# Thresholded attention and a GELU layer on one core: conversion steps made whole, and the first weight loads moved behind the rows of pair two

## The chip, the cores and the metric

The kernel runs on one core of a Trainium2 chip. Time is the device time of one execution in microseconds (us), and kernels are compared by the median of their runs. TensorE is called PE, and PEld where it loads weights; VectorE is DVE, ScalarE is ACT, GpSimd is POOL. SyncE is SP: it only issues transfers here. Each of ACT, POOL and SP has a DMA queue of its own.

## What is computed

The inputs are q, k and v of shape (8, 8, 576, 64) in single precision, a threshold tau, and two weight matrices, 512 x 2048 and 2048 x 512. The weights come in double precision, eight bytes a number.

```
scores = q @ k^T / 8
keep scores that are >= max(scores) - tau, the others count as -1e9
attn = exp(scores - max); attn /= (sum(attn) + 1e-9)
x = (attn @ v), heads side by side: 4608 tokens x 512
out = gelu(x @ w_in) @ w_out, gelu exact
```

## The kernel before, in words

The attention works on pairs of heads: 32 pairs, four to each of the eight batches. The 576 queries of a pair go in five slots: four chunks of 128, and one for the last 64 queries of both heads. So a batch of four pairs has 20 slots. The first batch has an order of its own: first the chunks 0 and 1 of all four pairs (slots 0 to 7), then the chunks 2, 3 and the rest, pair by pair (slots 8 to 19).

What a slot does, in the order in which it is written:

1. `scores` (L410): matmuls of queries and keys into two score banks in PSUM, one for each head. There are only two of them, so the next slot's scores wait for this slot's masking.
2. `softmax_head`: for each head the maxima (L422, DVE), the threshold from them (L425, POOL) and the exponentials (L427, ACT). Between the first maxima and the first threshold, `add_low_bits(True)` puts one addition of converted weights (L226, POOL), the newest that is due. After `softmax_head` a plain `add_low_bits()` puts the others.
3. `turn_qk_early`, in slots 0, 2 and 4: the next pair's q and k are turned by PE (L326, and L336 for the last rows) and copied by ACT (L329 to L343).
4. Sums with v of an earlier slot (L546, L570), their division, and in the second half of the batch first matmuls of the big layers (L638).
5. `turn_p_early` (L356, L363, L372): the masked exponentials of the slot before are turned.
6. `softmax_tail` (L443, DVE): masking by the threshold and the row sums, in one operation.
7. Loads that are due, and `convert`, with a budget in ns for this slot's share of weight conversion.

Weights come as 32 pieces of 512 columns, 512 KB each as they lie in memory. `load_piece` (L183) issues the load of the next piece. It goes to a slot of `xall` or, for every other piece, to a part of `turned_p`. Each piece takes these steps from double to single precision: ACT makes `power` from the high words (L202) and a part of the result from the low words (L203); DVE shifts `power` (L210) and brings in the sign (L212); POOL adds the two (L226). `conversions` is a generator that issues these steps, ACT's two pieces ahead of DVE's, and yields what each costs in ns. `convert` adds 1200 (slots 1 and 2) or 1900 ns (later slots) to a debt and takes steps until the debt is used up; slot 19 takes all that are left. As written, the generator yields 340 after L210 and 720 after L212, and only after that second yield is the piece entered in `sums_due`, from which `add_low_bits` takes, and the next load issued.

At the start, `load_early` loads q and k of the pairs 0, 1 and 2: q on the SP queue, k of pair 0 on ACT's, of pair 1 on POOL's, and all of pair 2 on SP's, into slots of `xall`. The rows 512 to 575 of a pair are loaded apart, as a tail. Pieces 0 and 1 follow pair 0's k on ACT's queue, pieces 2 and 3 pair 1's k on POOL's. `load_v_early` and `load_early(3)` then load pair 0's v, pair three's q and k, and pair 1's v on SP's queue. After `turn_qk_early(0)` the generator is started, with ACT's first two steps.

After the first batch, PE alternates between attention and the big layers in an order laid down by `goal` and `fill`; the last ten blocks of tokens are multiplied at the end in a scheme with fewer products (L826).

Of the kernel before, what the change touches and what calls it, by code (L numbers as in the profile page):

```python
# [18 lines left out]
def kernel(  # L19
# [28 lines left out]
    nc = tc.nc  # L48
# [53 lines left out]
    def x_slot(want=None):  # L102
        i = max(x_free) if want is None else want
        x_free.remove(i)
        return i
# [8 lines left out]
    def x_rows(i):  # L114
        return xall[:, i, :, :].rearrange("p c t -> p (c t)")
# [45 lines left out]
    def load_piece(eng=nc.sync):  # L161
        k = loaded[0]
        if k == len(pieces):
            return
        staged = k % 2 and k < len(pieces) - LATER
        if wide and not staged and not x_free:
            return
        dst, src = pieces[k]
        loaded[0] += 1
        if not wide:  # L170
            nc.sync.dma_start(dst, src)
            converted[0] += 1
            load_piece()
            return
        slot = []
        if staged:

            half, at = divmod(k // 2 % 4, 2)
            raw = pd[half].bitcast(U32)[:, at * 2 * PIECE:(at + 1) * 2 * PIECE]
        else:  # L180
            slot = [x_slot()]
            raw = x_rows(slot[0]).bitcast(U32)
        eng.dma_start(raw, src.bitcast(U32))  # L183
        raws.append((dst, raw, slot))

    def conversions():

        vec = nc.vector
        ahead = []
        done = 0
        while raws or ahead:
            if raws:
                dst, raw, slot = raws.pop(0)
                lo, hi = (raw.rearrange("p (f w) -> p f w", w=2)[:, :, i] for i in range(2))  # L200
                power = gp.tile([P, PIECE], U32, tag="g", name="power")
                nc.scalar.activation(power.bitcast(FP32), hi.bitcast(FP32), AF.Copy, bias=0.0, scale=2.0 ** -112)  # L202
                nc.scalar.activation(dst.bitcast(U32), lo, AF.Copy, bias=0.0, scale=2.0 ** -29)  # L203
                ahead.append((dst, hi, power, slot))
                yield 0
            if len(ahead) == LATER and done == len(pieces) - LATER:
                yield None
            if len(ahead) == 2 or not raws:
                dst, hi, power, slot = ahead.pop(0)
                vec.tensor_scalar(power, power, 3, 0x7FFFFFF8, op0=ALU.logical_shift_left, op1=ALU.bitwise_and)  # L210
                yield 340
                vec.scalar_tensor_tensor(power, hi, 0x80000000, power, op0=ALU.bitwise_and, op1=ALU.bitwise_or)  # L212
                x_free.extend(slot)
                yield 720
                sums_due.append((dst.bitcast(U32), power))
                load_piece()
                done += 1
                yield 0

    sums_due = []  # L220

# [7 lines left out]
    conv = {"steps": None, "debt": 0.0}  # L229

    def convert(ns, least=0):

        if conv["steps"] is None:
            conv["steps"] = conversions()
        conv["debt"] += ns
        while conv["debt"] > 0 or least > 0:
            took = next(conv["steps"], None)
            if took is None:
                return
            conv["debt"] -= took  # L240
            least -= took
# [31 lines left out]
    def load_early(p):  # L273
        b, hp = divmod(p, HP)
        s = st[p] = {}
        for name, src in (("q", q), ("k", k)):

            if p == 2:
                at = s[name + "_slot"] = x_slot()
                t = x_rows(at)[:, 0:2 * (NC + 1) * D].rearrange("p (e c d) -> p e c d", e=2, d=D)  # L280
            else:
                t = ld.tile([P, 2, NC + 1, D], FP32, tag=name, name=name)
            s[name] = t
            eng = (nc.scalar, nc.gpsimd)[p] if p < 2 and name == "k" else nc.sync
            for e in range(2):
                rows = src[b, 2 * hp + e, 0:MAIN, :]
                if name == "q":
                    eng.dma_start(t[:, e, 0:NC, :].rearrange("p (g c) d -> p g (c d)", c=2),
                                  rows.rearrange("(g p c) d -> p g (c d)", p=P, c=2))
                else:  # L290
                    eng.dma_start(t[:, e, 0:NC, :], rows.rearrange("(p t) d -> p t d", p=P))
            eng.dma_start(t[0:TAIL, :, NC, :], src[b, 2 * hp:2 * hp + 2, MAIN:S, :].rearrange("e s d -> s e d"))

    def load_v_early(p):
        b, hp = divmod(p, HP)
        t = st[p]["v"] = v_sb[p % 4]
        for e in range(2):
            nc.sync.dma_start(t[:, e, 0:NC, :], v[b, 2 * hp + e, 0:MAIN, :].rearrange("(p t) d -> p t d", p=P))
            nc.sync.dma_start(t[e * TAIL:(e + 1) * TAIL, e, NC, :], v[b, 2 * hp + e, MAIN:S, :])
# [735 lines left out]
        assert not beside  # L1035

    load_early(0)
    for _ in range(2):
        load_piece(nc.scalar)
    some = const.tile([P, 1], FP32, name="some")  # L1040
    nc.vector.tensor_scalar(some, tau_sb, 0.0, None, op0=ALU.is_ge)
    nc.vector.tensor_scalar(q_scale, some, SCALE, None, op0=ALU.mult)
# [2 lines left out]
    nc.vector.tensor_scalar(tau_eff, tau_sb, lift, None, op0=ALU.max)  # L1045
    nc.scalar.activation(warm[:, 1:2], warm[:, 0:1], AF.Exp)
    load_early(1)
    for _ in range(2):
        load_piece(nc.gpsimd)
    load_early(2)  # L1050
    for t in q_tail + [t[:, :, NC, :] for t in v_sb]:
        nc.vector.memset(t, 0.0)
    turn_qk_early(0)
    conv["steps"] = conversions()
    next(conv["steps"])
    load_v_early(0)
    load_early(3)
    load_v_early(1)
# [167 lines left out]
```

## Time and profile before

| | before |
|---|---|
| median of 3 runs | 1341.14 us (1337.87 to 1342.4) |
| profiled execution | 1338.39 us |
| its span | 1336.6 us |
| PE busy | 1318.4 us |
| DVE busy | 1042.8 us |
| ACT busy | 604.7 us |
| POOL busy | 640.2 us |
| L210, 32 in the first 140 us | 16.8 us, 525 ns each |
| L212, 32 in the first 140 us | 26.8 us |
| L226, 32 in the first 140 us | 42.5 us |

Busy time is summed over the span. A line of the timeline gives the start in us, the duration in us, the engine, the line of the kernel, the operation, what it writes and reads, the shape, the count, and in brackets the engine's idle time before it and what ended it. An end that is written as "DMA" is a landing transfer. In a table by stage, each engine's busy time is followed by the number of its instructions, and the last columns are the granted PE clock as a share of full speed, the mean busy share of the DMA engines, and GB/s.

### The profile page before, as it was taken

How to read it: one execution, taken by the hardware profiler on the slowest of the kernel's cores; microseconds unless marked ns; L12 is line 12 of the kernel's file. 1: busy time of each engine (PE TensorE's matmuls, PEld its weight loads, DVE VectorE, ACT ScalarE, POOL GpSimd, SP SyncE). 2: the span in 40 equal slices, each digit the busy share in tenths (PEclk: the TensorE clock that was granted, in tenths of full speed). 3: DMA queues.
4: the chain of work that ended last, by engine and by line, in shares of the span. 5: the costliest groups of instructions: out<-in, count | busy, mean ns of one | idle time of the engine just before them, and what ended most of it. 6: DMA issues, size and time to landing. Idle time of an engine off the chain costs nothing.

```text
span 1336.6 us, 19968 instructions
## 1 busy us (share of the span) xinstructions
PE 1318.4 (99%) x6362; PEld 895.1 (67%) x6362; DVE 1042.8 (78%) x2005; ACT 604.7 (45%) x1029; POOL 640.2 (48%) x1063
## 2 busy tenths in 40 slices
PE   8899999999999999999999999999999999999998
PEld 6677466466466466466466557568787787877877
DVE  6977777788888888888888888783857698386775
ACT  7877457268367358348448438332211113211120
POOL 4655454555555555546545551235264503635530
PEclk9999999999999999999999999999999999999999
DMA  7662566776776786786786775400000130000003
GB/s 234 211 171 50 124 151 141 168 184 152 176 188 151 180 202 153 179 211 154 168 222 159 163 188 121 106 9 1 1 0 1 40 103 17 0 1 0 1 0 79
DMA packets 209784, 152.42 MB, mean 114 GB/s; under 512 B 113360, under 2 KB 193088, under 8 KB 209680
## 3 DMA queue, kind: packets, MB, share of 16 engines
q1 hardware_dynamic: 191680, 125.11, 39.7%
q0 software_dynamic: 17280, 24.69, 6.8%
q10 hardware_dynamic: 720, 1.34, 0.3%
q8 instruction: 52, 0.85, 0.3%
q14 instruction: 52, 0.43, 0.1%
HBM read 55.97 MB, written 12.52 MB: 51 GB/s over the span
## 4 chain that ended last, share of the span: by engine, by line
PE 93%; DMA 2%; ACT 2%; DVE 2%; issue 0%; SPq 0%; DVEq 0%; ACTq 0%
PE bank L826 34%; PE o_ps L653 17%; PE hT L638 16%; PE sc L410 13%; PE xT L546 11%; ACT p L427 1%; DMA xall<-in_moe_w_in_dram 1%; DMA q<-in_q_dram 1%; DMA x<-xall 0%; DVE nmx L422 0%; PE tr L356 0%; DVE power L212 0%; ACT pT L363 0%; DVE power L210 0%; DVE p L443 0%
## 5 line engine op out<-in xcount | busy, mean ns | idle before, releaser
L427 ACT ACTIVATE p<-sc,nmx 128x576 f32<-128x576 f32 x288 | 201.7, 738 | 276.6 <-DVE nmx L422 276.4
L443 DVE SCALAR_TENSOR_TENSOR p<-sc,thr,p 128x576 f32<-128x576 f32 x288 | 225.2, 815 | 74.3 <-ACT p L427 70.2
L425 POOL TENSOR_SCALAR thr<-nmx,tau_eff 128x1 f32<-128x1 f32 x288 | 84.2, 293 | 355.8 <-DVE nmx L422 347.0
L638 PE MATMUL hT<-xall,w_in 128*128 128x256 f32 x1024 | 241.9, 386 | 0.0
L422 DVE TENSOR_REDUCE nmx<-sc 128x1 f32<-128x576 f32 x288 | 205.3, 749 | 45.0 <-PE sc L410 43.5
L653 PE MATMUL o_ps<-w_out,g 128*128 128x512 f32 x512 | 236.8, 603 | 0.0
L638 PEld LDWEIGHTS hT<-xall,w_in 128*128 128x128 f32 x1024 | 189.4, 190 | 50.1 <-issue 23.0
L708 DVE TENSOR_TENSOR c<-c,bank 128x320 f32<-128x320 f32 x304 | 146.9, 486 | 34.0 <-PE bank L826 20.6
L708 DVE TENSOR_TENSOR o<-o,bank 128x256 f32<-128x256 f32 x240 | 99.6, 418 | 93.8 <-PE bank L826 88.8
L653 PEld LDWEIGHTS o_ps<-w_out,g 128*128 128x128 f32 x512 | 93.1, 190 | 109.1 <-issue 106.5
L410 PE MATMUL sc<-kT,qT 64*128 64x288 f32 x960 | 159.5, 429 | 2.0 <-DVE p L443 1.9
L546 PE MATMUL xT<-pT,v 128*64 128x320 f32 (+1 forms) x1240 | 159.6, 410 | 0.7 <-DVE pT L367 0.5
L507 DVE STREAM_TRANSPOSE turned_p<-p 128x1152 f32<-128x1152 f32 x112 | 154.4, 1378 | 3.9
L410 PEld LDWEIGHTS sc<-kT,qT 64*128 64x128 f32 x960 | 91.5, 186 | 74.9 <-issue 60.9
L546 PEld LDWEIGHTS xT<-pT,v 128*64 128x64 f32 x1240 | 86.5, 137 | 71.5 <-issue 10.8
L826 PE MATMUL bank<-w_out,c 128*128 128x256 f32 x480 | 120.2, 381 | 0.5 <-DVE o L708 0.5
L269 POOL DMA_DIRECT2D v<-in_v_dram x208 | 110.8, 536 | 3.8 <-issue 1.7
L826 PEld LDWEIGHTS bank<-w_out,c 128*128 128x128 f32 x480 | 90.0, 190 | 18.7 <-DVE o L708 2.9
L879 ACT ACTIVATE c<-c 128x320 f32<-128x320 f32 (+1 forms) x80 | 46.9, 624 | 114.6 <-DVE c L708 114.5
L708 POOL TENSOR_TENSOR c<-c,g 128x320 f32<-128x320 f32 (+1 forms) x40 | 50.6, 1272 | 67.5 <-DVE c L708 67.5
L826 PE MATMUL bank<-t_out,c 128*128 128x256 f32 x320 | 82.8, 381 | 0.0
L826 PE MATMUL bank<-t_out,g 128*128 128x256 f32 x320 | 82.1, 379 | 0.0
(182 smaller groups left out, 1771.5 us busy)
## 6 DMA issues: line engine op xcount, KB each, us to landing
pT<-turned_p SPq DMA_DIRECT2D x448, 160.0 KB, 3.5
pT<-pd_tail SPq DMA_DIRECT2D x112, 80.0 KB, 2.9
q<-in_q_dram POOLq DMA_DIRECT2D x104, 72.0 KB, 3.4
k<-in_k_dram POOLq DMA_DIRECT2D x104, 72.0 KB, 2.9
inv<-turned SPq DMA_DIRECT2D x54, 128.0 KB, 3.9
v<-in_v_dram POOLq DMA_DIRECT2D x156, 40.0 KB, 3.1
out_dram<-o SPq DMA_DIRECT2D x40, 128.0 KB, 2.3
xall<-in_moe_w_out_dram SPq DMA_DIRECT2D x9, 512.0 KB, 4.3
```

Of the source, the lines that this page charges most:

```text
L269: eng.dma_start(t[r:P:4, e, 0:n, :], rows[:, r * KR:r * KR + n, :])
L410: nc.tensor.matmul(sc[e][:, h, 0:HALF], lhsT=lhsT, rhs=s["kT"][rows, at:at + HALF], start=True, stop=True)
L422: nc.vector.tensor_reduce(nmx[:, e:e + 1], sc, axis=AXIS.XY, op=ALU.max, negate=True)
L425: nc.gpsimd.tensor_scalar(thr[:, e:e + 1], nmx[:, e:e + 1], -1.0, tau_eff, op0=ALU.mult, op1=ALU.subtract)
L427: nc.scalar.activation(w[:, e * S:(e + 1) * S].rearrange("p (h s) -> p h s", h=2), sc, AF.Exp, bias=nmx[:, e:e + 1], scale=1.0)
L443: nc.vector.scalar_tensor_tensor(row, sc[e][:, :, 0:HALF], thr[:, e:e + 1], row, op0=ALU.is_ge, op1=ALU.mult, accum_out=den[e])
L507: nc.vector.transpose(turned_p[:, :, i // 2, 0:NB, i % 2 * Q:(i % 2 + 1) * Q], w.rearrange("p (e b i) -> p e b i", e=2, i=Q))
L546: nc.tensor.matmul(to, lhsT=s["v"][:, e, c, :], rhs=rhs, start=(c == 0), stop=(c == KR - 1))
L638: nc.tensor.matmul(hT[:, j % 2, :], lhsT=w_in_sb[c][:, j * P:(j + 1) * P], rhs=x_blk[n][:, c, :], start=(c == 0), stop=(c == N_DM - 1))
L653: nc.tensor.matmul(o[:, 0:d_model], lhsT=g[j][:, m * P:(m + 1) * P], rhs=w_out_sb[j], start=(j == 0), stop=(j == N_DF - 1))
L708: eng.tensor_tensor(out, a, b, op=ALU.add)
L826: nc.tensor.matmul(to, lhsT=l, rhs=r, start=start and k == 0, stop=k == len(pairs) - 1, skip_group_check=not start)
```

## The change

Two things are changed. In `conversions`, L210 and L212 of a piece form one step of 1060 ns, and the piece is entered in `sums_due`, and the next load issued, before the generator yields. At the start, the first four pieces are loaded on SP's queue, after pair two's rows, and the generator is no longer started there: its first steps come with `convert` in slot 1.

```diff
             if len(ahead) == 2 or not raws:
                 dst, hi, power, slot = ahead.pop(0)
                 vec.tensor_scalar(power, power, 3, 0x7FFFFFF8, op0=ALU.logical_shift_left, op1=ALU.bitwise_and)
-                yield 340
                 vec.scalar_tensor_tensor(power, hi, 0x80000000, power, op0=ALU.bitwise_and, op1=ALU.bitwise_or)
                 x_free.extend(slot)
-                yield 720
                 sums_due.append((dst.bitcast(U32), power))
                 load_piece()
                 done += 1
-                yield 0
+                yield 1060
...
     load_early(0)
-    for _ in range(2):
-        load_piece(nc.scalar)
...
     load_early(1)
-    for _ in range(2):
-        load_piece(nc.gpsimd)
     load_early(2)
+    for _ in range(4):
+        load_piece(nc.sync)
     for t in q_tail + [t[:, :, NC, :] for t in v_sb]:
         nc.vector.memset(t, 0.0)
     turn_qk_early(0)
-    conv["steps"] = conversions()
-    next(conv["steps"])
     load_v_early(0)
     load_early(3)
     load_v_early(1)
```

## The prediction

> **What bounds the kernel now.** I read the chain of waits first (93% TensorE), then busy time by stage, because the change touches only the first attention batch and the start.
>
> ```profile
> PE 93%; DMA 2%; ACT 2%; DVE 2%; issue 0%; SPq 0%; DVEq 0%; ACTq 0%
> ```
>
> By stage:
>
> ```profile
> 0.00:75.00 75.00, 65.82 (x557) 49.72 (x557) 59.13 (x132) 60.70 (x128) 41.28 (x66) 0.98 0.68 222
> ...
> 75.00:140.00 65.00, 62.44 (x388) 46.27 (x388) 48.18 (x98) 51.53 (x102) 33.92 (x56) 1.00 0.38 86
> 140.00:876.00 736.00, 735.09 (x3516) 439.59 (x3515) 624.72 (x1123) 402.26 (x616) 371.35 (x758) 1.00 0.71 165
> ```
>
> The rows are stage, length, busy time of PE, PEld, DVE, ACT, POOL, clock, DMA share, GB/s. TensorE is idle 9.2 us of the first 75, 2.6 us of the next 65, and 0.9 us of the 736 after that. Its instructions have the same order in both kernels. So whatever is gained or lost before 140 us reaches the end one for one, and only about 12 us of idle time, and what a lowered clock adds, is to be had. That is the frame of the forecast.
>
> Then the timeline of the first 75 us. Slots are numbered by their maxima (L422): slot 2 at 19.11, 6 at 44.02, 7 at 50.40, 8 at 55.41, 11 at 71.84.
>
> ```profile
> 8.40 0.33 PE L336 MATMUL tr<-ident,q 64*64 64x64 f32 x4 [1.44 <-DMA q<-in_q_dram]
> ...
> 10.00 0.66 ACT L202 ACTIVATE power<-xall 128x512 f32<-128x512 f32 x1
> 10.57 0.65 ACT L203 ACTIVATE w_in<-xall 128x512 uint32<-128x512 uint32 x1
> 11.24 1.37 ACT L427 ACTIVATE p<-sc,nmx 128x576 f32<-128x576 f32 x2
> ```
>
> The first scores wait 1.44 us for the tail rows of pair 0's q, and piece 0 is converted on ACT while ACT has little else.
>
> ```profile
> 41.79 1.29 POOL L226 TENSOR_TENSOR w_in<-power,w_in 128x512 uint32<-128x512 uint32 x1 [0.72 <-DVE power L212]
> ...
> 41.93 1.45 DVE L210 TENSOR_SCALAR power<-power 128x512 uint32<-128x512 uint32 x1 [0.22 <-ACT power L202]
> ...
> 48.42 1.32 POOL L226 TENSOR_TENSOR w_in<-power,w_in 128x512 uint32<-128x512 uint32 x1 [0.79 <-DVE power L212]
> ...
> 48.65 1.66 DVE L212 SCALAR_TENSOR_TENSOR power<-turned_p,power 128x512 uint32<-128x512 uint32 x1
> ```
>
> And the stages around the gap that follows:
>
> ```profile
> 46.00:48.00 2.00, 1.57 (x7) 1.58 (x8) 1.97 (x6) 2.00 (x7) 1.38 (x2) 0.62 0.51 180
> 48.00:50.00 2.00, 2.00 (x11) 1.37 (x9) 1.97 (x3) 1.74 (x4) 1.32 (x1) 0.53 0.31 66
> ```
>
> L210 usually takes 0.42 and L212 0.69. When an addition on POOL started just before, they take 1.45 and 1.66, and end with it. TensorE is idle from 44.09 to 46.42, and its clock is then 0.62 and 0.53.
>
> [...] L210 and L212 stretch as shown, while maxima under an addition (55.41) keep their 0.7 us. [...] The trace shows 0.53 after a gap of 2.33 us, and 1.00 after gaps of 1.34 and 1.44 us (73.1, 6.96). [...] pair 0's q tail needed some 6.6 us from issue to landing beside the pieces on two other queues, pair three's on the SP queue alone 3.5 us.
>
> **The change part by part.**
>
> *(a) Pieces 0 to 3 leave the ACT and POOL queues and enter SP's behind pair two.* ACT loses issues of 0.60 and 0.41 us; its table load (4.95) can start near 2.4. POOL loses 0.58 and 0.56 where it waits until 11.05 anyway: worth nothing. The q tail, issued at 1.75, should land near 1.75 + 3.5 = 5.3, at worst as today, 8.4. Below 7.0 it no longer matters, since TensorE turns k until 6.96. Then the tail turns at 7.0, the kT copy ends at 7.69 as now, the held-back scores run at 8.05 instead of 9.38, maxima at 8.85 instead of 10.18. The exponentials now start as soon as the first maximum is done: 9.62 instead of 11.24, 1.6 us earlier, of which ACT's copies for pair one keep 1.5. Pair one's q, which landed at 11.0, must be there by 9.25; with 2 MB fewer bytes beside it I take that as given.
>
> SP issues four more pieces, some 2.1 us, before pair 0's v, pair three's q and k, and pair one's v. These are needed at 24.18 and 29.72 and today were issued by 12.3 and 21.6: covered, unless over 3 us slower. SP's own issues sum to about 10 us up to the last piece; 2.1 MB at the 350 GB/s seen at 10 to 14 us then take 6 us. So the pieces land between about 11 and 17 us (an estimate from these rates). They are needed from 16.3 on, one each 1.15 us: just covered. Two later pieces move ahead of pair three's v and of pair four's rows; those are used over 10 us after they land.
>
> *(b) Piece 0's conversion moves behind slot 0.* On ACT, L202 and L203 (0.58 us each in sequence) leave 10.0 to 11.2, where only about 0.3 us of them delayed anything, counted in (a), and join slot 1, where ACT is busy without a break from 15.39 to 27.3. DVE gets a fourth operation there: L210 and L212 of piece 1 must follow its L202. Before slot 2: L202 of piece 1 ends 19.65, L210 19.7, L212 20.15, maxima 20.75, exponentials 21.45, all less 1.5, so 19.95 instead of 20.08. **Start and delay cancel: 0.1 us gained.**
>
> *(c) Whole steps.* No slot ends between L210 and L212 any more, and an addition enters at once. So the newest addition follows the slot's last L212, under the maxima. Counting the 340, 720 and 1060 through the slots: before, the newest addition ran into an L210 or L212 in slots 6, 7, 11, 12, 15 and 17, for 1.03, 0.97, 1.00, 0.96, 0.49 and 0.96 us; after, in none. Price: the addition (1.3 us) starts 0.23 after the maxima do, so the threshold (0.3) behind it is ready at 1.85 and the masking (L443) starts at 1.90 instead of 1.63 in most slots: 0.27 each. Behind the masking wait DVE's next conversions and TensorE's next scores, which need its score banks. Slots 2, 8, 13 and 18 get an L212 from the slot behind, 0.61 late there, given back one to five slots on. The second addition of a slot falls under the masking, and ends about when L210 follows (3.4 after the maxima); it costs up to 0.2, taken as 0. L473 still stretches an L210 by 0.3 to 0.5 as today.
>
> Following the dependences by slot, with 1.48 from masking start to the next conversion and 1.06 per step: ACT's 0.35 us wait for a piece at 30.92 goes, since that piece is issued sooner. Maxima of slot 6 at 44.02 - 0.45 - 1.03 = 42.54. Masking 44.44, two steps, slot 7 at 48.03 instead of 50.40; TensorE's gap shrinks to about 1 us, so the lowered clock should not come, and today's scores until 50.37 do not hold it. Slot 8: 51.4 + L473's 0.5 + wait for L202, 54.0 instead of 55.41 (the borrowed L212). Slot 11: 69.6 instead of 71.84. Scores of slot 12, today 74.44 waiting for masking, at about 72.5: **2.0 us gained.** Behind it TensorE is nearly full; slot 17's 0.96, less 0.27, shortens the 0.84 us gap at 113.47: **0.5 more.** Sum 0.1 + 1.9 + 0.5 = 2.5 us.
>
> The profiled execution took 1338.39 (span 1336.6 and 1.8 around it), so it becomes 1335.9; the median of three runs, 1341.14, is 2.75 above it, and becomes 1338.6. I take differences, not the level.
>
> **Rivals.**
> 1. *Contention was the path in full, and the start keeps its gain.* Pieces arrive early, ACT absorbs piece 0, thresholds hide. For: 3.97 us of stretches lie before 74 us. Against: ACT has no gap from 15.39 to 27.3. Start 1.5, stretches 3.97 less 0.6 handed on, clock 1.0: 5 to 6 us, 1335.5.
> 2. *The thresholds replace the stretches.* 0.27 in ten slots, a second addition stretching L210 by 0.2 in eight, is 4.3, against 3.97 and 0.5: no change, 1341.
> 3. *Pieces arrive late: slower.* SP is held for some 3.5 us at 12.3 today; if it is held before the pieces, they are issued at 13 to 15 and, with the 6 us to landing of the page, land at 19 to 21. ACT then stands in L202 in slot 1 with slot 2's exponentials queued behind, DVE in L210 with the maxima behind. Each us beyond 16.3 costs one; beyond 18.8 the whole is slower. At 21.5 it is 5.2 lost against 2.5: 1344. For: the chain shows SP's pieces at 28 to 41 us. Against: ACT's queue has only 0.35 us of waits for them.
>
> That the change does nothing is excluded by the changed order on DVE and POOL; that its parts cancel is rival 2.
>
> **How the numbers follow.** About 0.3% (4 us) is what a measurement can tell here. Own forecast 0.47 (gain 1 to 4.5, a part above 4), rival 1 0.22, rival 2 0.18, rival 3 0.13 (a third of it, 0.04, beyond 4 us). Faster by over 0.3%: 0.22 and 0.06 of mine, 0.28; slower 0.04, and 0.07 of my own case for a cost of this kind that I overlooked, 0.11; within 0.61. Range 1334.5 to 1343.0: rival 1 down to a gain of 6.6, and rival 3 up to a loss of 1.9.
>
> **What would show it.** Right: L336's tail within 0.3 us of 7.0; L202 first near 16.3 without a DMA wait; slot 2's maxima within 0.4 of 19.2; L210 and L212 at 0.42 and 0.69 except beside L473; slot 7 near 48.0, clock 1.00 from 46 to 50; scores of slot 12 near 72.5. Wrong: ACT waiting for a piece before 27 us; L443 waiting for thresholds by more than 0.4; idle before the maxima that TensorE ends; a new low clock elsewhere.

## The result, and the profile after

| | before | after |
|---|---|---|
| median of 22 runs | 1340.59 us | 1337.51 us |
| lowest and highest | 1337.87, 1343.45 us | 1335.05, 1339.92 us |
| profiled execution | 1338.39 us | 1338.74 us |
| its span | 1336.6 us | 1336.9 us |
| DVE busy in it | 1042.8 us | 1038.9 us |
| POOL busy in it | 640.2 us | 633.6 us |

The ratio of the medians is 0.9983, with an interval of 0.9976 to 0.9990: a gain of 3.1 us, which is a gain, but a small one (0.17%). The two profiled executions hardly show it: before's lies 2.2 us below its median, after's 1.2 us above its own. So the traces say which stalls went and came, and only the medians say what they were worth.

The chain of waits and the stages after, in the columns of the prediction's fences:

```profile
PE 92%; DVE 2%; ACT 2%; DMA 2%; SPq 1%; issue 1%; POOL 0%; ACTq 0%; DVEq 0%
```

```profile
0.00:75.00 75.00, 65.70 (x557) 48.83 (x558) 56.84 (x132) 61.53 (x129) 37.16 (x65) 0.98 0.70 222
75.00:140.00 65.00, 62.85 (x388) 46.22 (x388) 46.06 (x96) 51.30 (x101) 31.44 (x55) 1.00 0.38 86
140.00:876.00 736.00, 734.66 (x3516) 438.83 (x3515) 624.65 (x1122) 402.34 (x616) 371.41 (x758) 1.00 0.71 165
```

DVE lost 2.3 us of busy time in the first stage and 2.1 in the second, since no L210 or L211 is stretched by an addition any more (in slot 6 L210 takes 0.43 us and not 1.45). TensorE's busy time, 65.70 against 65.82 us, and the mean clock are as they were: in this execution what was gained in one place of the first 75 us was lost in another.

Where it was gained, in the timeline of after (L334, L210, L211 and L224 here are L336, L210, L212 and L226 of before):

```profile
7.36 0.33 PE L334 MATMUL tr<-ident,q 64*64 64x64 f32 x4
...
43.29 0.43 DVE L210 TENSOR_SCALAR power<-power 128x512 uint32<-128x512 uint32 x1 [0.23 <-ACT power L202]
43.75 0.69 DVE L211 SCALAR_TENSOR_TENSOR power<-turned_p,power 128x512 uint32<-128x512 uint32 x1
44.36 1.42 DVE L420 TENSOR_REDUCE nmx<-sc 128x1 f32<-128x576 f32 x2
44.59 1.27 POOL L224 TENSOR_TENSOR w_in<-power,w_in 128x512 uint32<-128x512 uint32 x1 [2.17 <-DVE power L211]
45.84 0.56 POOL L423 TENSOR_SCALAR thr<-nmx,tau_eff 128x1 f32<-128x1 f32 x2
46.18 0.82 DVE L441 SCALAR_TENSOR_TENSOR p<-sc,thr,p 128x576 f32<-128x576 f32 x1 [0.33 <-POOL thr L423]
```

The tail rows of q no longer wait for a transfer. In slot 6 the addition starts 0.23 us after the maxima and lies under them: L210 and L211 take 0.43 and 0.69, not 1.45 and 1.66. The price stands in the last line: the masking waits 0.33 us for the threshold and starts 1.82 us after the maxima. In the first 140 us such waits were 1.2 us in 3 places before; the waits of after:

```profile
DVE p L441 <- POOL thr L423: 6.8, 15, 1.0
```

Where it was lost. The stages of two places, after; the clock is the third number from the end:

```profile
22.00:24.00 2.00, 1.36 (x9) 1.06 (x11) 1.97 (x6) 1.96 (x7) 1.43 (x2) 0.91 0.68 158
24.00:26.00 2.00, 2.00 (x11) 0.91 (x10) 0.80 (x2) 1.95 (x6) 1.26 (x1) 0.50 0.97 360
26.00:28.00 2.00, 2.00 (x18) 1.17 (x16) 1.69 (x4) 1.80 (x3) 0.58 (x2) 0.74 1.07 385
...
48.00:50.00 2.00, 2.00 (x26) 1.52 (x28) 1.93 (x5) 2.00 (x4) 0.17 (x1) 1.00 0.22 78
```

The lowered clock of 46 to 50 us is gone. A new one has come at 23 to 27 us, where before had 1.00. The same place before:

```profile
22.00:24.00 2.00, 1.88 (x14) 1.25 (x13) 1.47 (x4) 1.94 (x7) 1.30 (x2) 1.00 0.45 135
24.00:26.00 2.00, 1.93 (x16) 1.11 (x16) 1.49 (x3) 1.98 (x6) 1.43 (x3) 1.00 0.56 159
```

In the timeline before, the scores of slot 3 follow without a longer pause:

```profile
22.87 1.24 PE L410 MATMUL sc<-kT,qT 64*128 64x288 f32 x8
```

The timeline of after there, with the cause in brackets:

```profile
17.61 0.43 DVE L210 TENSOR_SCALAR power<-power 128x512 uint32<-128x512 uint32 x1 [0.72 <-ACT power L202]
...
20.60 1.40 ACT L425 ACTIVATE p<-sc,nmx 128x576 f32<-128x576 f32 x2 [0.17 <-DVE nmx L420]
22.64 0.81 PE L354 MATMUL tr<-ident,p 128*128 128x128 f32 x5 [1.53 <-ACT qT L327]
23.37 2.08 PE L408 MATMUL sc<-kT,qT 64*128 64x288 f32 x8
```

The scores of slot 3 (L408) take 2.08 us; at full clock they took 1.24. In slot 1 ACT now converts three pieces and not two; DVE waits 0.72 us for the first of them and has one sign step (L211) more before slot 2's maxima. So slot 2's exponentials end at 22.00, and ACT's copy for pair two follows them. TensorE had come to slot 2 sooner, with scores at 16.30 instead of 17.20, and stands for 1.53 us until the copy is done. By the start of each slot's maxima:

| slot | 0 | 1 | 2 | 3 | 4 | 6 | 7 | 8 | 11 | scores of 12 |
|---|---|---|---|---|---|---|---|---|---|---|
| before | 10.18 | 14.60 | 19.11 | 24.14 | 30.58 | 44.02 | 50.40 | 55.41 | 71.84 | 74.44 |
| after | 9.54 | 13.69 | 19.82 | 25.47 | 32.58 | 44.36 | 49.79 | 55.75 | 71.50 | 74.29 |

After is 0.6 us ahead at slot 0 and 2.0 behind at slot 4; it gains that back by slot 12. From there to slot 21 and to the end the two take the same time to within half a microsecond.

### The profile page after: what moved, and what is told of

It reads as the page before. It is cut to its first block, busy times and chain, and to the rows that moved or that the text cites. A ratio compares the mean times of both kernels' runs of the same rounds, so it can differ in the third digit from the quotient of the medians.

```text
span 1336.9 us, 19969 instructions
## 1 busy us (share of the span) xinstructions
PE 1318.9 (99%) x6362; PEld 893.4 (67%) x6362; DVE 1038.9 (78%) x2005; ACT 605.4 (45%) x1029; POOL 633.6 (47%) x1061
## 4 chain that ended last, share of the span: by engine, by line
PE 92%; DVE 2%; ACT 2%; DMA 2%; SPq 1%; issue 1%; POOL 0%; ACTq 0%; DVEq 0%
PE bank L824 34%; PE o_ps L651 17%; PE hT L636 16%; PE sc L408 13%; PE xT L544 11%; ACT p L425 1%; DVE nmx L420 1%; DMA q<-in_q_dram 1%; PE tr L354 1%; DMA x<-xall 1%; DVE power L211 1%; DMA turned_p<-in_moe_w_in_dram 0%; ACT pT L361 0%; DVE p L441 0%; DVE power L210 0%
## 5 line engine op out<-in xcount | busy, mean ns | idle before, releaser
L636 PE MATMUL hT<-xall,w_in 128*128 128x256 f32 x1024 | 242.0, 386 | 0.5 <-ACT g L603 0.5
L636 PEld LDWEIGHTS hT<-xall,w_in 128*128 128x128 f32 x1024 | 189.3, 190 | 50.8 <-issue 23.0
L408 PE MATMUL sc<-kT,qT 64*128 64x288 f32 x960 | 159.9, 431 | 2.1 <-DVE p L441 1.6
L408 PEld LDWEIGHTS sc<-kT,qT 64*128 64x128 f32 x960 | 91.0, 186 | 75.8 <-issue 60.1
```

Of the source, the lines that this page charges most:

```text
L408: nc.tensor.matmul(sc[e][:, h, 0:HALF], lhsT=lhsT, rhs=s["kT"][rows, at:at + HALF], start=True, stop=True)
L636: nc.tensor.matmul(hT[:, j % 2, :], lhsT=w_in_sb[c][:, j * P:(j + 1) * P], rhs=x_blk[n][:, c, :], start=(c == 0), stop=(c == N_DM - 1))
```

## The experiments

The theory when they began: the gain comes from the stretches of slots 6 to 17 and the clock that falls with them; the moved loads by themselves give almost nothing; and the new low clock behind slot 2 takes back a part. Ratios are to the kernel before on the same chip, with their intervals. The first four ran on one chip (before 1338.67), the next three on a second (1338.52), the last three on a third (1340.16).

**Each part alone.** The loads on SP's queue with the old steps; the new steps with the old loads; both again.

```diff
 # new loads, old steps (from after)
+                yield 340
                 vec.scalar_tensor_tensor(power, hi, 0x80000000, power, op0=ALU.bitwise_and, op1=ALU.bitwise_or)
                 x_free.extend(slot)
+                yield 720
                 sums_due.append((dst.bitcast(U32), power))
...
-                yield 1060
+                yield 0
```

The other is the rest of the change: before, with the two early yields taken out and `yield 1060` at the end.

> The loads of the first four pieces behind pair two's rows and the late start of the conversions, but the yields of before (340, 720, 0). Own theory (the start's gain and the conversion moved into slot 1 cancel; the whole steps make the gain): 0 to 0.5 us under before, slot 2's maxima within 0.4 of 19.1 us, and L210 and L212 stretched in slots 6, 7 and 11 as before. Rival (the start keeps its gain): 1.4 us or more under before. Rival (ACT's fuller slot 1 leaves TensorE idle there, and its clock drops): 1 to 2 us over before, with a clock near 0.5 at 22 to 28 us.

> Whole steps entered at once, but the first four pieces on ACT's and POOL's queues and the early start of the conversions as before. Own theory: nearly all of the gain, 2 to 3 us under before, no L210 or L212 stretched by an addition, slot 7's maxima near 48.5 us. Rival (the gain comes from the start): under 0.7 us. Rival (thresholds behind additions take it back): 0 to 0.5 us.

> The changed kernel unaltered, for a second profile and its time beside the other runs. Theory of a clock that falls in slot 2 in some executions only: a profile in which the clock stays 1.00 from 22 to 28 us has slot 4's maxima near 30.5 instead of 32.58 and scores of slot 12 near 72.5 instead of 74.29, and takes about 1336.5. Rival (the clock falls there in every execution): the same profile as the first, slot 4 at 32.6. Time against before: 3.1 us less, as in the 22 runs.

| | median us | ratio | slot 4 | slot 7 | slot 8 | scores of 12 |
|---|---|---|---|---|---|---|
| loads alone | 1337.31 | 0.9987 [0.9981, 0.9994] | 30.89 | 50.05 | | 74.08 |
| steps alone | 1337.07 | 0.9987 [0.9978, 0.9996] | 31.10 | 48.30 | 54.28 | 72.83 |
| both | 1337.43 | 0.9991 [0.9983, 0.9999] | 32.77 | | | 74.50 |

On this chip both parts gain some 1.5 us alone (1.4 and 1.6), and together no more than one of them: they don't add. The loads alone were expected to be worth half a microsecond at most, and the steps alone 2 to 3; both were misses. The second profile of after has the low clock behind slot 2 again (0.97, 0.50 and 0.68 in the three stages from 22 to 28 us), so the first execution was not alone with it; and its gain is 1.2 us here, not the 3.1 of the first measurement. The steps alone do what the prediction described: no L210 or L211 is stretched by an addition, slot 7 starts at 48.30, and no stage has a low clock. With the loads alone the stretches stay, here the one of slot 6:

```profile
41.76 1.44 DVE L210 TENSOR_SCALAR power<-power 128x512 uint32<-128x512 uint32 x1 [0.21 <-ACT power L202]
```

and with them the low clock: 0.50 from 48 to 50 us, behind a pause of 2.34 us as before.

The low clock behind slot 2 needs both parts. With the loads alone ACT also has three pieces in slot 1, but DVE has one sign step less; TensorE's pause there is 1.25 us, with the steps alone 0.66, and the clock stays at 1.00 in both.

**A smaller budget**, so that slot 1 gets only one whole step, not two.

```diff
-        convert(0 if n == 0 else 1200 if n < 3 else 1900 if n < BATCH - 1 else 1e9)
+        convert(0 if n == 0 else 1000 if n < 3 else 1900 if n < BATCH - 1 else 1e9)
```

> The changed kernel with a budget of 1000 instead of 1200 ns in slots 1 and 2: slot 1 has two of ACT's piece conversions instead of three and one of DVE's instead of two; the lost one is made good in slot 4. If ACT's fuller slot 1 is what eats the start's gain: slot 2's maxima near 18.6 instead of 19.8 us, TensorE's gap before 22.6 under 0.7 us, no low clock at 22 to 28, and 1 to 2 us under the changed kernel. If ACT is full up to slot 4 anyway: slot 4 at the same time as in the changed kernel with a full clock (30.5), and no more than 0.5 us of difference.

1338.67 us, 0.9998 [0.9990, 1.0007]: no gain at all over before, though the low clock behind slot 2 was gone in its profile. The expected 1 to 2 us under the changed kernel did not come. The debt that slot 1 left had shifted. A second step had gone into slot 4, where ACT also copies pair three's q and k. The timeline of that kernel:

```profile
36.07 0.43 DVE L210 TENSOR_SCALAR power<-power 128x512 uint32<-128x512 uint32 x1 [1.78 <-ACT power L202]
...
37.14 1.42 DVE L420 TENSOR_REDUCE nmx<-sc 128x1 f32<-128x576 f32 x2
```

The maxima of slot 5 came 7.29 us after those of slot 4, 29.85 to 37.14, against 4.83 in after. DVE stands in L210 with the maxima behind it, as rival 3 had it, only for ACT and not for a transfer. But this is not where the gain went: the scores of slot 12 start at 72.56 us, 1.7 us sooner than in after, or 1.1 counted from slot 0's maxima (8.91 us here). It went behind them. From there to the scores of slot 21 this kernel needs 58.93 us and after 57.35, with two waits of TensorE, one for ACT and one for a masking:

```profile
119.88 1.13 PE L636 MATMUL hT<-xall,w_in 128*128 128x256 f32 x4 [1.32 <-ACT g L603]
...
131.49 1.95 PE L408 MATMUL sc<-kT,qT 64*128 64x288 f32 x8 [0.78 <-DVE p L441]
```

A debt that carries over moves the steps of all later slots, so this run shows what a lighter slot 1 does up to slot 12 and not what it is worth in the end.

**Is it the gap before slot 3?** The same matmuls that turn pair two's k are issued twice, so TensorE has 1 us of extra work just ahead of the gap.

```diff
+            if p == 2 and name == "k":
+                for c in range(NC):
+                    for e in range(2):
+                        nc.tensor.matmul(tr[e * D:(e + 1) * D, c, :], lhsT=t[:, e, c, :], rhs=ident, start=True, stop=True)
```

> The changed kernel, but TensorE turns pair two's k twice (16 matmuls more, the same values), in the gap that it has in slot 2 while ACT converts three pieces. If the low clock at 23.3 to 26.8 us comes from that gap: clock 1.00 there, slot 4's maxima near 31.2 instead of 32.6 to 32.8, scores of slot 12 near 73 instead of 74.3 to 74.5, and 1 to 1.5 us under the changed kernel. Rival (the clock falls for another reason, or the late slot 4 comes from ACT): slot 4 stays at 32.6, and the time stays within 0.3 us of the changed kernel.

1336.38 us, 0.9981 [0.9975, 0.9988]. The timeline of this kernel, whose lines stand four lower than after's:

```profile
22.47 0.80 PE L358 MATMUL tr<-ident,p 128*128 128x128 f32 x5 [0.67 <-ACT qT L331]
23.20 1.24 PE L412 MATMUL sc<-kT,qT 64*128 64x288 f32 x8
```

The gap is 0.67 us in place of 1.53, the scores take 1.24 us again, and no stage of it is below 1.00. From slot 0 to slot 4 it needs 22.05 us (9.36 to 31.41), after 23.04 (9.54 to 32.58). More work on TensorE made the start 1.0 us shorter: what cost time there was the clock, not the wait. It holds beyond the one profile: all 22 executions of this kernel have a mean clock of 0.999 or 1.000, while 17 of the first 22 of after have 0.998.

**Even steps.** The budget is replaced by a list, how many whole steps each slot gets: one each in slots 1 and 2, one in the turning slot 4, one in slots 13, 17 and 18. It ran once on after and once on the old loads with the new steps.

```diff
+    STEPS = [0, 1, 1, 2, 1, 2, 2, 2, 2, 2, 2, 2, 2, 1, 2, 2, 2, 1, 1]
...
-        convert(0 if n == 0 else 1200 if n < 3 else 1900 if n < BATCH - 1 else 1e9)
+        conv["debt"] = 0.0
+        convert(1060 * STEPS[n] if n < BATCH - 1 else 1e9)
```

> The changed kernel with whole steps given out by a list instead of the debt: one in slots 1, 2, 4, 13, 17 and 18, two in the others. Slot 1 gets one step less, slot 9 one more, and one moves from slot 17 to 18. If the fuller slots 1 and 17 eat the gain: slot 2's maxima near 18.1 to 18.8, no low clock at 22 to 28, slot 5 near 34.5, scores of slot 12 near 72, no 0.5 us wait of TensorE for ACT's copy (L603) near 120, maxima of slot 20 near 126.5: 2.5 us under the changed kernel, 4 under before. Rival (slot 9's second step costs what slot 1 saved): 0 to 0.7 us under the changed kernel.

> The same list of whole steps, but loads and the early start of the conversions as before the change. If what the moved loads bring at the start (0.6 to 1.3 us earlier first maxima) is kept when slot 1 is not overfull, this is that much slower than the kernel with the same list and the new loads. Rival (the early conversion of piece 0 in slot 0 is worth as much): within 0.3 us of it.

Against after, slot 1 has one step less, slot 9 one more, and one has moved from slot 17 to 18. On after: 1335.79 us, 0.9977 [0.9971, 0.9984], 2.7 us under before where 4 were expected; slot 4 at 30.53, slot 7 at 47.73, scores of slot 12 at 72.86, no low clock. On the old loads: 1337.45 us, 0.9991 [0.9981, 1.0000], scores of slot 12 at 74.85. So where slot 1 isn't overfull, the moved loads are worth about 1.7 us. Drawing the 22 and 14 runs anew many times (resampling) gives 0.2 to 3.3 us as a 95% interval, so the 1.5 that the prediction worked out for the start fits, but is not confirmed by it.

**What the place under the maxima is worth.** All additions go behind both thresholds of a slot.

```diff
-            if e == 0:
-                add_low_bits(True)
```

> The changed kernel with all additions of a slot behind its two thresholds, none under the maxima. Own theory (an addition under the maxima costs the masking about 0.2 us, and elsewhere runs into L210 and L212): masking starts 1.63 after the maxima again instead of 1.82, but in slots with two additions the second one ends about 4.2 after the maxima and stretches an L210 by 0.6 to 1.0, so slots 6 to 12 take 0.4 to 0.8 us more each, and the time is 2 to 4 us over the changed kernel. Rival (waiting for thresholds is dearer than the stretches): 0.5 to 1.5 us under the changed kernel.

> The changed kernel unaltered, beside the two others on one chip. 1.2 to 3.1 us under before, as in its two measurements so far; its low clock at 23 to 27 us again.

> The list of whole steps with the new loads again, on one chip with the changed kernel. If it is the better one: 1 to 2 us under the changed kernel and 2.5 to 3.5 under before. Rival (the earlier difference was one of chips): within 0.5 us of the changed kernel.

| | median us | ratio |
|---|---|---|
| additions behind the thresholds | 1341.31 | 1.0007 [1.0000, 1.0014] |
| after, unaltered | 1337.42 | 0.9984 [0.9977, 0.9992] |
| even steps on after | 1336.33 | 0.9972 [0.9964, 0.9981] |

Without an addition under the maxima the whole gain is gone and slightly more: 3.9 us. Slot 6 in the timeline of that kernel:

```profile
45.44 0.82 DVE L439 SCALAR_TENSOR_TENSOR p<-sc,thr,p 128x576 f32<-128x576 f32 x1
45.57 2.50 POOL L224 TENSOR_TENSOR w_in<-power,w_in 128x512 uint32<-128x512 uint32 x2
...
46.92 1.44 DVE L210 TENSOR_SCALAR power<-power 128x512 uint32<-128x512 uint32 x1
```

The masking starts 0.19 us sooner after the maxima (43.81 to 45.44) than in after, but two additions in a row reach to 48.07, past the masking, and hit L210. The 3.9 us are not stretches alone. This profile has the low clock of after at 22 to 26 us and a second one, behind a pause of 2.23 us; the clock is the third number from the end:

```profile
60.00:62.00 2.00, 2.00 (x11) 1.34 (x10) 1.97 (x3) 2.00 (x6) 1.29 (x2) 0.51 0.22 86
62.00:64.00 2.00, 2.00 (x22) 1.40 (x20) 1.97 (x5) 0.69 (x2) 0.07 (x1) 0.64 0.39 76
```

This pair is the direct test of rival 2: a threshold 0.19 us late is far cheaper than L210s that are 1 us longer (1.44 us, not 0.43), with the second low clock beside them (0.51 and 0.64).

The even list was 1.1 us below after on this chip, and 3.8 below before. Resampling the 22 runs of each gives 0.3 to 2.3 us for the difference to after, so it beats after here, but by how much is not settled; on the second chip after itself did not run.

## Why the prediction was right, and where its steps failed

**The frame held.** From the scores of slot 21, at 131.45 us before and 131.64 after, the rest takes 1205.2 and 1205.3 us. In the twelve profiled executions it is 1204.0 to 1206.3 us, so what is won or lost in the first batch reaches the end one for one, within about a microsecond of scatter, and it could only be a few microseconds.

**(a) The start.** The tail was turned at 7.36 (forecast 7.0), no transfer held ACT before 27 us, and SP issued the pieces from 8.10 to 10.1; so rival 3 did not happen. Maxima of slot 0 came at 9.54 where 8.85 was forecast: the transposes at the very start ran slower in this execution, 0.42 us for a single one in place of 0.27. In the third run of after, with 0.27, the maxima came at 9.04. The rest is in the sum: in after all scores of slot 0 wait for ACT's copies of the tail (0.50 us), and the maxima start 1.24 us after them (8.30 to 9.54), where the forecast has 0.8. In medians, the loads gave 1.4 us alone.

**(b) Piece 0 in slot 1.** From slot 1 to slot 2 after needs 6.13 us, by the forecast's working 6.15, and before 4.51. The start's gain is used up here, as stated.

**(c) The stretches.** All six went, and the low clock at 46 to 50 us with them. The threshold costs less than forecast, 0.19 us and not 0.27. One reading in the forecast is loose: a stretched L210 or L212 doesn't end with the addition. In its own lines L210 ends 0.30 us behind it (43.38 and 43.08) and L212 0.57 us (50.31 and 49.74). The sums use the full durations and stand.

**The first step that failed** is one that the forecast left out. It followed (b) on ACT and DVE and did not ask what TensorE does meanwhile. TensorE's pause of 1.53 us came from there and from the whole steps of (c) in the same slot, and with it half clock. The forecast had named "a new low clock elsewhere" as a sign against it. It was there, in all three profiled executions of after and in the kernel with the additions behind the thresholds, which has the same slot 1 (pauses of 1.53 to 1.56 us). It was in none of the kernels in which slot 1 had less to convert or the pause was filled; the longest pause there is the 1.25 us of the loads alone. From the maxima of slot 2 to those of slot 4, before needs 11.47 us and after 12.76. With the pause filled it is 11.76 (19.65 to 31.41), so 1.0 of the 1.3 us is the clock. The rest is a wait: with whole steps, the last L210 of slot 3 comes in the same slot as the L202 that it needs, and stood 1.60 us for it. With the steps alone and full clock the maxima of slot 4 came 6.95 us after those of slot 3, against 6.44 before. The forecast put this wait in words for slot 8 and at nothing here; it is 0.3 to 0.5 us.

So slot 7 came at 49.79 instead of 48.0 and the scores of slot 12 at 74.29 instead of 72.5 (74.50 and 73.73 in the other two profiled executions of after). The steps alone, whose slot 1 is lighter, had 48.30 and 72.83, close to what the forecast gave to both parts.

**The second step that failed** is the "0.5 more" behind slot 12. From the scores of slot 12 to those of slot 21 before took 57.01 us and after 57.35. The gap of 0.84 us at 113.47 is gone, but the second whole step in slot 17 holds up ACT, and TensorE waits for it later. The waits of after, from 75 to 131 us:

```profile
PE hT L636 <- ACT g L603: 0.5, 1, 0.5
```

With one step in slot 17, in the even list, this wait is gone, and the same stretch takes 56.63 us.

**Why the total still fits.** In the first profiled execution of each kernel the gain at slot 12 is 0.15 us and not 2.0, and yet the median gains 3.1. The mean granted clock of each execution tells a part of it. On the third chip of the experiments, the executions sorted by it (number, and their median):

| mean clock | before | after |
|---|---|---|
| 0.995 | 11: 1342.29 us | none |
| 0.996 | 12: 1340.42 us | none |
| 0.997 | 9: 1340.08 us | 1: 1338.61 us |
| 0.998 | 23: 1339.21 us | 10: 1337.83 us |
| 0.999 and 1.000 | 4: 1338.1 us | 11: 1337.1 us |

At the same clock after is some 1.0 to 1.4 us ahead, and the rest of the 2.7 is that 23 of 59 executions of before have 0.996 or less and none of after. On the first chip, where the gain is 1.2 us, it is 4 of 49, and after is 0.7 us ahead at 0.998 (8 executions against 28). Where half clock shows in the stages of the first 70 us of a profile, it lasts 3.4 us: in after from the three stages above (0.09 + 0.50 + 0.26) x 2 / 0.5, in before from 46 to 50 us (0.38 + 0.47) x 2 / 0.5, and the stages of four more profiles give the same (the loads alone, the two other profiles of after, and twice the additions behind the thresholds). One such spell takes 0.0013 from the mean (3.4 x 0.5 / 1337), an estimate; by it the executions of before at 0.995 have some two more than those at 0.998, and they are 3.1 us longer. A single value is less sharp than that: the clock also falls at the very end, in the profile of before from 1333.4 us on (0.65 from 1333 to 1334, then 0.50), after the last matmul at 1331.6, and that costs nothing but takes up to as much from the mean. Among the stalls that the change takes away is the one of 2.34 us that ends at 46.42 in before, with 0.62 and 0.53 from 46 to 50 us. Its own new pause has one such spell behind it in each profiled execution, and yet the mean clock rises: over all executions the mean is 0.9970 before and 0.9986 after on the third chip, 0.9977 and 0.9985 on the first.

So 2.5 us were forecast and 3.1 measured, and the agreement is partly luck. On the first chip the steps alone gain 1.6 us and the loads alone 1.4, and both together 1.2, so that 1.7 are missing. About 1.0 of it is the new low clock, which needs both parts. The two waits for ACT, in slot 3 and at L636, don't explain the rest, since the steps alone have them too; it stays open. And the executions with a mean clock of 0.996 or less are gone, which the forecast, made from one execution, did not count. After has 1337.4 to 1337.5 us in all three measurements, while before has 1338.7 to 1340.6, so the size of the gain (1.2, 2.7 and 3.1 us) is set by before.

It also stays open in which places before loses the clock in its longer executions. How much of each part's 1.5 us is clock can be told roughly from the first chip: the loads alone are 1.2 us ahead of before at a mean of 0.998 (14 executions against 28), the steps alone 1.3 at 0.999 (9 against 5). By these few executions most of each part's gain is shorter work. For the loads the trace does not bear this out: their profiled execution is only 0.4 us ahead at the scores of slot 21 (131.09).

**The rivals.** Rival 1, the full 5 to 6 us, did not come about; the best that was reached is the even list's 3.8, where slot 1 has a whole step less. Of the 3.97 us of stretches that rival 1 puts before 74 us, 0.96 lie at 76.47. Rival 2 is refuted by the kernel with the additions behind the thresholds. Rival 3 had the right picture of a DVE that stands in L210 with the maxima behind it, as in slot 4 of the kernel with the smaller budget, but ACT's conversions bring it about there and the transfers don't.

## What to carry to other kernels

When work is moved into a stage, follow it on every engine, the idle one too: behind a new pause of 1.53 us on TensorE the clock fell to 0.50, and that made up 1.0 of the 1.3 us lost there. Work that stretches another engine's instructions belongs under one that it leaves alone, even if something small behind it gets later: here an addition, beside which L210 took 1.45 us and not 0.43, under the maxima, which take 1.42 us a pair with it and without. Where the gain is a few spells of half clock, 3.4 us each here, one profile can't show it; many runs and their mean clock can.

## What the hardware showed that I had not expected

- Pauses of 1.53 to 1.56 us on TensorE were followed by 3.4 us of half clock in every profiled execution of after, while pauses of 1.34 and 1.44 us in before left the clock at 1.00. But the length of the pause does not decide alone. In the even list on the old loads the clock stayed at 1.00 behind a longer one, 1.94 us, as its timeline and its stages show:

```profile
9.15 0.33 PE L334 MATMUL tr<-ident,q 64*64 64x64 f32 x4 [1.94 <-DMA q<-in_q_dram]
```

```profile
6.00:8.00 2.00, 1.21 (x22) 0.97 (x16) 1.64 (x8) 1.24 (x3) 0.00 (x0) 1.00 0.90 274
8.00:10.00 2.00, 0.85 (x10) 0.60 (x10) 0.00 (x0) 0.34 (x2) 0.00 (x0) 1.00 1.04 346
```

No run shows what else decides.

- With 1 us of extra matmuls the kernel had 0.9981 of the time before, no worse than after's 0.9983, 0.9991 and 0.9984 (after was not run on the same chip): here that work, which only keeps TensorE busy, cost nothing that shows.
- The first transposes of an execution took 0.27 us in some and 0.42 in others of the same kernel; the first maxima of after came at 9.54, 9.70 and 9.04 us.
